# Own tiles for decays and inverses in the first early stage, and its loads in parts

## The chip, the cores and the metric

The kernel runs on one core of one Trainium2 chip. The metric is the device time of one execution in microseconds (us), taken from the kernel's first to its last work on that core; lower is better. Several timed runs are given by their median, and one more execution was profiled.

## The reference

Three stages follow each other. The first is a linear recurrence over 768 steps for 4 x 8 heads with a 40 x 40 state; its output, as 3072 rows of 320, goes through a dense two-layer network and then through a network of 8 experts, where each row goes to the expert with the largest logit.

```python
for t in range(S):                       # S = 768, state: B x H x D x D, D = 40
    y[:, :, t] = einsum('bhd,bhde->bhe', rt, state)
    Sa = einsum('bhde,bhe->bhd', state, at)
    state_decay = state * wt[:, :, None, :] - einsum('bhd,bhe->bhde', Sa, bt)
    state = state_decay + einsum('bhd,bhe->bhde', vt, kt)
x = y.transpose(0, 2, 1, 3).reshape(3072, 320)
h = x @ w_in;  g = maximum(0.01 * h, h);  x = g @ w_out       # 320 -> 2048 -> 320
e = argmax(x @ w_gate, axis=1)                                # 8 experts, capacity 768
out[i] = gate[i] * (relu(x[i] @ w1[e]) @ w2[e])
...
```

The weights w_in and w_out arrive as 64-bit floats; the kernel reads their bits and makes 32-bit floats of them.

## The kernel before

**Stages.** The recurrence is cut into 12 pieces of 64 steps for each half of the heads. `early(e)` (6 of them, e = 0 to 5) prepares four such pieces, `c4` = 0 to 3, for 104 used partitions and 8 head pairs: it loads decays w and the vectors a, b, k (`early_load`, one row of 2057 floats for each of 104 partitions: 521 of w, 512 each of a, b and k), makes running products of the decays with a scan (`eW`, line 439) and of their inverses backwards (`eWi`, line 448), scales a, b and k by them (lines 444, 453, 454), writes the decays, the scaled a, the inverses and the scaled k to DRAM (`dW`, `dA`, `dI`, `dK`: `put`, lines 443, 450, 451, 455), and multiplies b with a on TensorE into `Lt` (lines 463 and 465). When all four pieces are in `Lt`, it inverts the triangular matrices: three transposes (lines 475 and 478), 30 elimination steps of two VectorE instructions each (lines 483 and 485), and a short tail on TensorE into `Inv[e % 2]`.

`late_load(i)` and `late(i)` (48 of them) read back what `early` wrote, for half of the heads of one piece; `chain(i)` carries the state through piece i and writes to `xd`; `moe(v)` (12 of them) is the dense network on 256 rows. `convert` makes 32-bit weights of w_out and w_in chunk by chunk: a load into a ring of three buffers (line 268), one ScalarE step (line 277), four or five VectorE or GpSimd steps (lines 279 to 285) and the split into two parts (290, 391). Behind the last chain come the experts (`Phase2`).

**Around the change.** In `early(0)` all four loads are issued ahead (five transfers, as the third is cut in two). The four pieces share one tile `s.eW` for the decays and one tile `s.eWi` for the inverses; a piece can write them only when the transfers to `dW` and `dI` of the piece before have read them. The raw data lie in `s.eL[0]`, in `s.eL[1]` (the same memory as `P` and `I11`, which the elimination uses), in `s.Inv[1]` and in a tile of the conversion's room `cv`; k of the third piece lies in `s.FG[2]`.

`clear(2)` fills `FG[2]`, `S`, `Inv[0]` and the logits with zeros on GpSimd (lines 225 to 227) and puts identities into `RI` on VectorE (line 231). `beyond` (line 247, ScalarE) looks at the raw decays for values out of range, two passes for each piece, and uses the place of the raw b as its output; in `early(0)` it comes behind the fourth `Lt`. The first transpose writes `P` and so waits for `beyond` of the second piece.

**Order.** Each engine and SP, which issues all of these transfers, works in order. The order on each engine is not that of the source: a planner at compile time ranks instructions by priority and by its own estimate of when each can start, so that the pieces, the late steps and the conversions come interleaved. `ahead(...)` raises the priority of `early(0)` and of the first chains; `issue_after` keeps `clear(2)`, the first late steps and `beyond` behind the last products of piece 3. `run` then merges 46 steps of `early(0)`, 8 of the first two `late`, and the conversion of the first 10 chunks of w_out.

```python
ld = [s.early_load(e, c4) for c4 in range(1 if e else 4)]
fW, fWi, fd = f(s.eW), f(s.eWi), f(s.ed1)
put(s.dW[ch], s.eW[q104])
put(s.dI[ch], s.eWi[q104, :, 1:65])
drain(take(ev, 12))
merge([(ev, 46), (l01, 8), (take(pr, P0), P0)])
```

Of the kernel before, what the change touches and what calls it, by code (L numbers as in the profile page):

```python
# [16 lines left out]
ALU = mybir.AluOpType  # L17
# [31 lines left out]
X0 = 1  # L49
# [35 lines left out]
class Room:  # L85
# [6 lines left out]
    def new(s, sh, dt=F32):  # L92
        s.n += 1
        n = f"{s.name}{s.n}"
        return s.p.tile(sh, dt, name=n, tag=n)
# [35 lines left out]
class Phase1:  # L131
# [272 lines left out]

    def early_load(s, e, c4):
        hh, C = e // 3, 4 * (e % 3) + c4
        t = s.eL0[c4] if e == 0 else s.eL[c4 % 2]
        src = s.I["e_wabk"][C, hh]
        if e == 0 and c4 == 2:
            k = s.FG[2].rearrange("q p two t -> q (p two t)")[0:104, 0:512]  # L410
            s.nc.sync.dma_start(t, src[:, 0:1545])
            s.nc.sync.dma_start(k, src[:, 1545:2057])
        else:
            k = t[:, 1545:2057]
            s.nc.sync.dma_start(t, src)
        v = lambda x: x.rearrange("q (p t) -> q p t", t=64)
        return t[:, 0:521], v(t[:, 521:1033]), v(t[:, 1033:1545]), v(k)

    def early(s, e):
        nc = s.nc  # L420
        ps = lambda: s.psum("m1") if e == 0 else s.psum("se")
        f = lambda t: t[0:104].rearrange("q p t -> q (p t)")
        ld = [s.early_load(e, c4) for c4 in range(1 if e else 4)]
        if e:
            yield
        for c4 in range(4):
            if c4 < 3 and e:
                ld.append(s.early_load(e, c4 + 1))
            ew, ea, eb, ek = ld[c4]
            q104 = slice(0, 104)  # L430
            fW, fWi, fd = f(s.eW), f(s.eWi), f(s.ed1)
            ch = 4 * e + c4
            put = nc.sync.dma_start
            s.clamp(ew, 520)

            if c4 == 0 and e:
                nc.vector.memset(s.ed1[:, :, 0:1], 1.0)
            for h in (0, 260):
                nc.vector.tensor_tensor_scan(fW[:, h:h + 260], ew[q104, h:h + 260], fd[:, h:h + 260], 0.0,
                                             op0=ALU.mult, op1=ALU.add)  # L440
            if c4 < 3:
                nc.vector.tensor_copy(s.ed1[q104, :, 0:1], s.eW[q104, :, 64:65])
            put(s.dW[ch], s.eW[q104])
            m1 = (nc.gpsimd if e or X0 & 1 else nc.vector).tensor_tensor(ea[q104], ea[q104], s.eW[q104, :, 0:64], op=ALU.mult)
            for h in (0, 1):
                c = slice(260 * h, 260 * h + 260)
                nc.vector.reciprocal(s.edr[q104, :, 64:65], s.eW[q104, 4 * h:4 * h + 4, 64:65])
                nc.vector.tensor_tensor_scan(fWi[:, c][:, ::-1], ew[q104, 1:521][:, c][:, ::-1], f(s.edr)[:, ::-1], 0.0,
                                             op0=ALU.mult, op1=ALU.add)
            put(s.dA[ch], ea[q104])  # L450
            put(s.dI[ch], s.eWi[q104, :, 1:65])
            yield
            m2 = (nc.gpsimd if e or X0 & 2 else nc.vector).tensor_tensor(eb[q104], eb[q104], s.eWi[q104, :, 1:65], op=ALU.mult)  # L453
            nc.gpsimd.tensor_tensor(ek[q104], ek[q104], s.eWi[q104, :, 1:65], op=ALU.mult)
            put(s.dK[ch], ek[q104])
            yield
            for _ in range(PD if e else 0):
                yield
            pB = ps().rearrange("q (p t) -> q p t", t=64)
            for p in range(8):  # L460
                for pi in range(2):
                    q = 64 * (1 - pi)
                    m3 = nc.tensor.matmul(pB[q:q + 64, p, :], lhsT=eb[q:q + 40, p, :], rhs=ea[q:q + 40, p, :],  # L463
                                          start=True, stop=True)
            m4 = nc.scalar.mul(s.Lt[:, c4], pB, -1.0)
            s.marks = m1, m2, m3, m4
            if e:
                s.beyond(ew, ch, eb)
            else:
                s.ew0.append((ew, eb))  # L470
            yield
# [8 lines left out]
        for j in range(1, 31):  # L480
# [3 lines left out]
                                    op=ALU.mult)  # L484
# [18 lines left out]
        for c in range(4):  # L503
            v = ps()[:, 0:256].rearrange("q (p t) -> q p t", t=32)
# [7 lines left out]
            v = ps()[:, 0:256].rearrange("q (p t) -> q p t", t=32)  # L512
# [217 lines left out]
    def run(s, p2):  # L730
# [25 lines left out]
        ev = ahead(s.tc, s.early(0), HE, HL, 52)  # L756
        room, wT, wg = s.room(0)
        i1 = s.Inv[1].rearrange("q c p t -> q (c p t)")
        s.eL0 = s.eL + [i1[0:104, 0:1545], s.chip.left[-1].new([104, 2057])]
        pr = s.convert(room, s.wout_chunks(wT, wg, s.banks["m2"], range(0, P0 + P1)))  # L760
        q = ExitStack()
        s.ew0 = []
# [674 lines left out]
```

## Time and profile before

| | |
|---|---|
| timed runs | 1274.09, 1274.45, 1287.01 us; median 1274.45 |
| the profiled execution, its own time | 1275.27 us |
| its span, first to last instruction | 1273.6 us |
| TensorE matmul busy | 1037.1 us, 81% of the span |
| VectorE (DVE) busy | 800.0 us, 63% |
| ScalarE (ACT) busy | 511.8 us, 40% |
| GpSimd (POOL) busy | 408.0 us, 32% |
| TensorE clock granted, mean | 0.942 of 2.4 GHz |
| moved by DMA | 149.52 MB, 117 GB/s over the span |

A busy share is a mean over stages with different limits, so a table by stretches of time is read with it. In a timeline a row is one instruction, or several alike in succession: its start, its length, engine, line of the code, operation, output and input; in brackets stands how long the engine had been idle before it and what it then was released by. SPq is the queue that issues transfers; its rows are the time of issuing, not of the transfer. "p", "cv" and the like are the rooms in which tiles lie, not single tiles.

### The profile page before, as it was taken

Reading aid. Unit: us, or ns where it says so; the run is one execution under the profiler, and the core shown is the slowest. Engines: PE = TensorE matmul, PEld = TensorE weight load, DVE = VectorE, ACT = ScalarE, POOL = GpSimd, SP = SyncE. Lnnn points to the kernel's source line nnn. Section 1 sums busy time; section 2 is a strip of 40 time slices with the busy share of each in tenths; the row PEclk is TensorE's granted clock in tenths of the full one; section 3 lists DMA queues with packets and bytes.
Section 4 is the critical chain, followed back from the end, with each engine's and each line's share of the span. In section 5 each row is a group of like instructions: output and inputs, shape, how many; then the busy total and the mean of one; then the engine's idle time right before and its main releaser. Section 6 shows DMA issues by size and latency. Waiting matters only on the chain. (4 is left out here: it accounts for less than half of the span.)

```text
span 1273.6 us, 31259 instructions
## 1 busy us (share of the span) xinstructions
PE 1037.1 (81%) x12429; PEld 937.0 (74%) x12429; DVE 800.0 (63%) x1677; ACT 511.8 (40%) x1113; POOL 408.0 (32%) x458
## 2 busy tenths in 40 slices
PE   1348943599889989898979988999998968979994
PEld 1336732478778878787878878889898958878983
DVE  4698597894696558855884579544368445543541
ACT  1334442345435354455434543444443235332330
POOL 3364453444321332234222332122242321432210
PEclk9999999999998989998987989999999988989998
DMA  6665265347534654466434644233233444533100
GB/s 166 155 169 138 76 170 153 110 100 181 147 93 101 151 148 104 108 163 162 104 102 105 166 118 113 71 96 91 73 110 103 132 125 126 183 104 106 32 21 20
DMA packets 215735, 149.52 MB, mean 117 GB/s; under 512 B 152820, under 2 KB 195979, under 8 KB 213061
## 3 DMA queue, kind: packets, MB, share of 16 engines
q1 hardware_dynamic: 211949, 138.47, 41.7%
q0 software_dynamic: 3504, 7.75, 2.0%
q8 instruction: 122, 2.00, 0.7%
q14 instruction: 160, 1.31, 0.4%
HBM read 112.39 MB, written 37.21 MB: 117 GB/s over the span
## 5 line engine op out<-in xcount | busy, mean ns | idle before, releaser
L707 PE MATMUL bank<-w,m 128*128 128x328 f32 x792 | 151.2, 329 | 1.6 <-ACT m L691 1.3
L1123 PE MATMUL bank<-p,p 128*128 128x256 f32 (+1 forms) x704 | 121.5, 332 | 33.3 <-issue 26.9
L1123 PEld LDWEIGHTS bank<-p,p 128*128 128x128 f32 x704 | 113.8, 208 | 37.8 <-issue 30.0
L686 PE MATMUL bank<-m,w 128*128 128x256 f32 x768 | 125.0, 309 | 7.2 <-DVE m L690 7.1
L707 PEld LDWEIGHTS bank<-w,m 128*128 128x128 f32 x792 | 122.2, 193 | 9.7 <-issue 2.5
L690 DVE TENSOR_TENSOR m<-bank,m 128x512 f32<-128x512 f32 x96 | 66.8, 696 | 87.5 <-ACT m L689 87.0
L686 PEld LDWEIGHTS bank<-m,w 128*128 128x128 f32 x768 | 106.5, 205 | 14.8 <-DVE m L690 7.6
L686 PE MATMUL bank<-g,w 128*128 128x256 f32 x768 | 114.9, 298 | 0.0
L693 POOL TENSOR_TENSOR m<-m,m 128x128 fp32r<-128x128 f32 x66 | 46.1, 699 | 192.1 <-ACT m L691 185.0
L686 PEld LDWEIGHTS bank<-g,w 128*128 128x128 f32 x768 | 101.4, 198 | 5.5 <-issue 2.0
L572 POOL TENSOR_SCALAR_AFFINE_SELECT p<-p 64x512 f32<-64x512 f32 x94 | 67.3, 716 | 104.4 <-ACT p L570 102.5
L689 ACT ACTIVATE m<-bank 128x512 f32<-128x512 f32 x96 | 57.2, 596 | 96.9 <-PE bank L686 66.7
L1140 PE MATMUL bank<-p,p 128*128 128x320 f32 x600 | 93.3, 311 | 0.0
L1140 PEld LDWEIGHTS bank<-p,p 128*128 128x128 f32 x600 | 88.5, 188 | 0.0
L463 PE MATMUL bank<-p 40*64 40x64 f32 x736 | 35.7, 262 | 57.0 <-POOL p L453 22.2
L485 DVE TENSOR_TENSOR p<-p 128x30 f32<-128x30 f32 (+9 forms) x180 | 74.1, 412 | 3.5
L463 PEld LDWEIGHTS bank<-p 40*64 40x64 f32 x736 | 32.1, 172 | 60.1 <-issue 25.6
L1146 POOL DMA_INDIRECT out<-p,p x25 | 25.0, 999 | 156.5 <-DVE p L1145 114.9
L483 DVE TENSOR_TENSOR p<-p 128x30 f32<-128x30 f32 (+9 forms) x180 | 69.5, 386 | 3.2
L707 PE MATMUL bank<-w,g 128*128 128x328 f32 x360 | 70.2, 340 | 0.0
L612 DVE TENSOR_TENSOR p<-bank,p 64x256 f32<-64x256 f32 x94 | 39.6, 421 | 46.5 <-PE bank L607 30.6
L1126 ACT ACTIVATE p<-bank 128x384 fp32r<-128x384 f32 (+2 forms) x88 | 36.3, 415 | 78.3 <-PE bank L1123 66.0
(234 smaller groups left out, 2199.4 us busy)
## 6 DMA issues: line engine op xcount, KB each, us to landing
p<-in_e_wabk SPq DMA_DIRECT2D x22, 835.7 KB
p<-in_w SPq DMA_DIRECT2D x8, 1280.0 KB
p<-di SPq DMA_DIRECT2D x96, 104.0 KB
p<-in_w SPq DMA_DIRECT2D x8, 1024.0 KB
p<-in_t_kb SPq DMA_DIRECT2D x48, 160.0 KB
dw<-p SPq DMA_DIRECT2D x24, 211.2 KB
di<-p SPq DMA_DIRECT2D x24, 208.0 KB
p<-dk SPq DMA_DIRECT2D x48, 104.0 KB
```

The source lines that it names most:

```text
L463: m3 = nc.tensor.matmul(pB[q:q + 64, p, :], lhsT=eb[q:q + 40, p, :], rhs=ea[q:q + 40, p, :], start=True, stop=True)
L483: nc.vector.tensor_tensor(tm, bc(P[:, j + 1:32, j:j + 1], [128, n, j]), bc(P[:, j:j + 1, 0:j], [128, n, j]), op=ALU.mult)
L485: s.step = nc.vector.tensor_tensor(P[:, j + 1:32, 0:j], P[:, j + 1:32, 0:j], tm, op=ALU.add)
L572: nc.gpsimd.affine_select(out=Fv, in_=Fv, compare_op=ALU.is_gt, fill=0.0, base=0, pattern=[[0, 4], [0, 2], [1, 64]], channel_multiplier=-1)
L612: nc.vector.tensor_tensor(F[q:q + 64, :, pi, 64:128], x[q:q + 64, :, 0:64], bc(s.nmask[q:q + 64, None, :], [64, 4, 64]), op=ALU.mult)
L686: nc.tensor.matmul(o, lhsT=l, rhs=r, start=(n == 0), stop=(n == 7))
L689: nc.scalar.mul(g, ph, 0.01)
L690: nc.vector.tensor_tensor(g, ph, g, op=ALU.max)
L693: nc.gpsimd.tensor_tensor(gL[:, GS:512], g[:, GS:512], gH[:, GS:512], op=ALU.subtract)
L707: nc.tensor.matmul(po[tt], lhsT=l[:, ts], rhs=r[:, fc, :], start=(fc == 0 and n == 0), stop=(fc == NFC - 1 and n == 2))
L1123: nc.tensor.matmul(o, lhsT=l, rhs=r, start=(i == 0), stop=(i == 7))
L1140: nc.tensor.matmul(po, lhsT=l[:, ts], rhs=r[:, fc, :], start=(fc == 0 and i == 0), stop=(fc == 7 and i == 2))
```

## The change

In `early(0)`, and only there, each piece gets a place of its own for the decays and for the inverses (`s.eW0`): piece 0 keeps `s.eW` and `s.eWi`, the decays of pieces 1 to 3 lie in `s.Inv[0]`, the inverses of pieces 1 and 2 in `s.FG[2]` and of piece 3 in a new tile. The scans, the products and the transfers to DRAM of a piece use its own place. `s.ed1` and `s.edr` stay shared.

The loads of the four pieces are cut into three parts each: w (521 floats a row), a and b together (1024), and k (512). The w and the a-and-b part of all four pieces are issued first, eight transfers, and then the four k parts: twelve transfers in place of five, of the same bytes. The raw data of pieces 2 and 3 move: piece 2 into a new tile and `Inv[1]`, piece 3 into a new tile and `Inv[1]`. The code for e = 1 to 5, the late steps, the chain and the conversions stay as they are.

```diff
--- before.py
+++ after.py
@@ -404,23 +404,27 @@
 
     def early_load(s, e, c4):
         hh, C = e // 3, 4 * (e % 3) + c4
-        t = s.eL0[c4] if e == 0 else s.eL[c4 % 2]
         src = s.I["e_wabk"][C, hh]
-        if e == 0 and c4 == 2:
-            k = s.FG[2].rearrange("q p two t -> q (p two t)")[0:104, 0:512]
-            s.nc.sync.dma_start(t, src[:, 0:1545])
-            s.nc.sync.dma_start(k, src[:, 1545:2057])
+        if e == 0:
+
+            w, ab, k = s.eL0[c4]
+            s.nc.sync.dma_start(w, src[:, 0:521])
+            s.nc.sync.dma_start(ab, src[:, 521:1545])
         else:
-            k = t[:, 1545:2057]
+            t = s.eL[c4 % 2]
+            w, ab, k = t[:, 0:521], t[:, 521:1545], t[:, 1545:2057]
             s.nc.sync.dma_start(t, src)
         v = lambda x: x.rearrange("q (p t) -> q p t", t=64)
-        return t[:, 0:521], v(t[:, 521:1033]), v(t[:, 1033:1545]), v(k)
+        return w, v(ab[:, 0:512]), v(ab[:, 512:1024]), v(k)
 
     def early(s, e):
         nc = s.nc
         ps = lambda: s.psum("m1") if e == 0 else s.psum("se")
         f = lambda t: t[0:104].rearrange("q p t -> q (p t)")
         ld = [s.early_load(e, c4) for c4 in range(1 if e else 4)]
+        if e == 0:
+            for c4 in range(4):
+                nc.sync.dma_start(s.eL0[c4][2], s.I["e_wabk"][c4, 0][:, 1545:2057])
         if e:
             yield
         for c4 in range(4):
@@ -428,7 +432,8 @@
                 ld.append(s.early_load(e, c4 + 1))
             ew, ea, eb, ek = ld[c4]
             q104 = slice(0, 104)
-            fW, fWi, fd = f(s.eW), f(s.eWi), f(s.ed1)
+            eW, eWi = (s.eW, s.eWi) if e else s.eW0[c4]
+            fW, fWi, fd = f(eW), f(eWi), f(s.ed1)
             ch = 4 * e + c4
             put = nc.sync.dma_start
             s.clamp(ew, 520)
@@ -439,19 +444,19 @@
                 nc.vector.tensor_tensor_scan(fW[:, h:h + 260], ew[q104, h:h + 260], fd[:, h:h + 260], 0.0,
                                              op0=ALU.mult, op1=ALU.add)
             if c4 < 3:
-                nc.vector.tensor_copy(s.ed1[q104, :, 0:1], s.eW[q104, :, 64:65])
-            put(s.dW[ch], s.eW[q104])
-            m1 = (nc.gpsimd if e or X0 & 1 else nc.vector).tensor_tensor(ea[q104], ea[q104], s.eW[q104, :, 0:64], op=ALU.mult)
+                nc.vector.tensor_copy(s.ed1[q104, :, 0:1], eW[q104, :, 64:65])
+            put(s.dW[ch], eW[q104])
+            m1 = (nc.gpsimd if e or X0 & 1 else nc.vector).tensor_tensor(ea[q104], ea[q104], eW[q104, :, 0:64], op=ALU.mult)
             for h in (0, 1):
                 c = slice(260 * h, 260 * h + 260)
-                nc.vector.reciprocal(s.edr[q104, :, 64:65], s.eW[q104, 4 * h:4 * h + 4, 64:65])
+                nc.vector.reciprocal(s.edr[q104, :, 64:65], eW[q104, 4 * h:4 * h + 4, 64:65])
                 nc.vector.tensor_tensor_scan(fWi[:, c][:, ::-1], ew[q104, 1:521][:, c][:, ::-1], f(s.edr)[:, ::-1], 0.0,
                                              op0=ALU.mult, op1=ALU.add)
             put(s.dA[ch], ea[q104])
-            put(s.dI[ch], s.eWi[q104, :, 1:65])
-            yield
-            m2 = (nc.gpsimd if e or X0 & 2 else nc.vector).tensor_tensor(eb[q104], eb[q104], s.eWi[q104, :, 1:65], op=ALU.mult)
-            nc.gpsimd.tensor_tensor(ek[q104], ek[q104], s.eWi[q104, :, 1:65], op=ALU.mult)
+            put(s.dI[ch], eWi[q104, :, 1:65])
+            yield
+            m2 = (nc.gpsimd if e or X0 & 2 else nc.vector).tensor_tensor(eb[q104], eb[q104], eWi[q104, :, 1:65], op=ALU.mult)
+            nc.gpsimd.tensor_tensor(ek[q104], ek[q104], eWi[q104, :, 1:65], op=ALU.mult)
             put(s.dK[ch], ek[q104])
             yield
             for _ in range(PD if e else 0):
@@ -756,7 +761,16 @@
         ev = ahead(s.tc, s.early(0), HE, HL, 52)
         room, wT, wg = s.room(0)
         i1 = s.Inv[1].rearrange("q c p t -> q (c p t)")
-        s.eL0 = s.eL + [i1[0:104, 0:1545], s.chip.left[-1].new([104, 2057])]
+        new = s.chip.left[-1].new
+        i0 = s.Inv[0].rearrange("q c p t -> q (c p t)")
+        fg = s.FG[2].rearrange("q p two t -> q (p two t)")
+        w = lambda x: x.rearrange("q (p t) -> q p t", t=65)
+        cut = lambda t: (t[:, 0:521], t[:, 521:1545], t[:, 1545:2057])
+        t3 = new([104, 1545])
+        s.eL0 = [cut(s.eL[0]), cut(s.eL[1]), (new([104, 521]), i1[0:104, 0:1024], i1[0:104, 1024:1536]),
+                 (t3[:, 0:521], t3[:, 521:1545], i1[0:104, 1536:2048])]
+        s.eW0 = [(s.eW, s.eWi)] + [(w(i0[:, 520 * k:520 * k + 520]), x) for k, x in
+                                   enumerate((w(fg[:, 0:520]), w(fg[:, 520:1040]), new([128, 8, 65])))]
         pr = s.convert(room, s.wout_chunks(wT, wg, s.banks["m2"], range(0, P0 + P1)))
         q = ExitStack()
         s.ew0 = []
```

## Rows read from the trace of the kernel before

**Rows 1.** Busy time by stretches; columns as the first line says
```profile
core 0: us, PE busy (x) PEld busy (x) DVE busy (x) ACT busy (x) POOL busy (x), PEclk, DMA share, GB/s
0.00:52.00 52.00, 11.27 (x180) 10.33 (x180) 23.46 (x43) 8.94 (x16) 17.93 (x29) 1.00 0.65 159
52.00:102.00 50.00, 24.38 (x132) 19.23 (x128) 47.19 (x120) 20.22 (x60) 26.97 (x24) 1.00 0.70 185
...
600.00:700.00 100.00, 89.50 (x1252) 78.59 (x1254) 73.47 (x148) 40.63 (x87) 26.51 (x30) 0.86 0.42 103
...
800.00:900.00 100.00, 97.92 (x1554) 87.95 (x1547) 46.09 (x90) 50.00 (x107) 23.67 (x30) 1.00 0.38 94
```

**Rows 2.** Timeline of DVE, 0 to 64 us
```profile
7.97 0.43 DVE L242 TENSOR_SCALAR p<-p 104x512 f32<-104x512 f32 x1 [7.97 <-DMA p<-in_e_wabk]
...
12.59 0.43 DVE L242 TENSOR_SCALAR p<-p 104x512 f32<-104x512 f32 x1 [3.38 <-DMA p<-in_e_wabk]
...
16.60 1.40 DVE L242 TENSOR_SCALAR p<-p 104x512 f32<-104x512 f32 x1
21.14 0.43 DVE L242 TENSOR_SCALAR cv<-cv 104x512 f32<-104x512 f32 x1 [3.14 <-DMA cv<-in_e_wabk]
...
32.15 0.70 DVE L439 TENSOR_TENSOR_SCAN p<-cv,p 104x260 f32<-104x260 f32 x1 [2.45 <-DMA dw<-p]
34.76 0.70 DVE L448 TENSOR_TENSOR_SCAN p<-p,p 104x260 f32<-104x260 f32 x1 [1.92 <-DMA di<-p]
...
44.02 0.70 DVE L448 TENSOR_TENSOR_SCAN p<-cv,p 104x260 f32<-104x260 f32 x1 [5.41 <-DMA di<-p]
...
45.70 0.69 DVE L453 TENSOR_TENSOR cv<-cv,p 104x512 f32<-104x512 f32 x1
...
52.11 1.94 DVE L475 STREAM_TRANSPOSE p<-p 128x1024 f32<-128x1024 f32 x1 [2.07 <-ACT p L247]
...
61.12 0.32 DVE L280 TENSOR_SCALAR cv<-cv 128x320 uint32<-128x320 uint32 x1
```

**Rows 3.** Groups of instructions by line and shape, 0 to 52 us
```profile
L231 DVE COPY p<-all 40x160 f32<-40x160 f32 x6 | 2.4, 400 | 0.1
...
L447 DVE RECIPROCAL p<-p 104x4 f32<-104x4 f32 x8 | 1.3, 168 | 0.1
```

**Rows 4.** Timeline of POOL, 0 to 52 us
```profile
16.03 1.68 POOL L454 TENSOR_TENSOR p<-p,p 104x512 f32<-104x512 f32 x1 [0.63 <-DVE p L448]
23.90 1.17 POOL L444 TENSOR_TENSOR p<-p,p 104x512 f32<-104x512 f32 x1 [6.19 <-DVE p L447]
...
42.07 1.22 POOL L225 MEMSET p<- 128x1344 f32 x1 [0.24 <-DMA dk<-p]
45.74 1.68 POOL L454 TENSOR_TENSOR cv<-cv,p 104x512 f32<-104x512 f32 x1 [2.46 <-DVE p L448]
```

**Rows 5.** Timeline of SP, 0 to 54 us
```profile
0.83 0.81 SPq L415 DMA_DIRECT2D p<-in_e_wabk  x2
...
31.11 0.90 SPq L451 DMA_DIRECT2D di<-p  x1
...
47.45 0.31 SPq L455 DMA_DIRECT2D dk<-cv  x1
...
53.39 1.30 SPq L268 DMA_DIRECT2D cv<-in_w_out  x3
```

**Rows 6.** Timeline of ACT, the first conversion of w_out
```profile
57.88 0.49 ACT L277 ACTIVATE cv<-cv 128x320 f32<-128x320 f32 x1 [0.99 <-DMA cv<-in_w_out]
```

**Rows 7.** Busy time by stretches of 10 us; columns as in group 1
```profile
50.00:60.00 10.00, 3.96 (x58) 3.20 (x52) 7.67 (x12) 7.83 (x20) 2.37 (x3) 1.00 0.80 207
...
90.00:100.00 10.00, 5.64 (x23) 4.47 (x23) 10.00 (x32) 3.40 (x12) 5.53 (x5) 1.00 0.98 238
```

**Rows 8.** Timeline of DVE, pieces 1 and 2 of the second early stage
```profile
175.41 0.41 DVE L242 TENSOR_SCALAR p<-p 104x512 f32<-104x512 f32 x1
...
188.07 0.42 DVE L242 TENSOR_SCALAR p<-p 104x512 f32<-104x512 f32 x1
```

## The prediction

> **What bounds the kernel now.** I read the busy table by stretches first, then the timelines of the engines at the front. From 600 us on TensorE is busy 90 to 98% of the time; in the first 52 us it is busy 11 us, and VectorE, which leads there, only 23.46 of 52 [rows 1]. From 52 to 102 VectorE is busy 47.19 of 50 us. So the front is a stretch of waits, what follows is a stretch of VectorE's work, and later TensorE sets the pace. Nothing in the program is tied to a point of time: all later work starts from what the first early stage leaves behind, so a microsecond won at the front is carried to the end unless something on the way is not ready earlier.
>
> VectorE's timeline shows what it waits for [rows 2]. First the loads: 7.97, 3.38 and 3.14 us ahead of three clamps. Then the stores: 2.45 us for a transfer to `dW`, 1.92 and 5.41 us for transfers to `dI`; that is the one tile for all pieces, read by the transfer while the next scan wants to write it. The last product of the stage ends at 45.70 + 0.69 = 46.39, the first transpose starts at 52.11, behind the products, `Lt` and `beyond` on ScalarE. The three later stores cost 9.8 us, and they also push the scans apart so that the loads and the stores alternate.
>
> **What the change removes: the waits for stores.** With a place for each piece no scan waits for a store. What remains is VectorE's own work: 23.46 us busy in the stretch less 2.4 us for the identities, 21.1 us, or 5.3 a piece [rows 1, 3]. That is measured with GpSimd beside it.
>
> **The loads in parts.** Two whole loads end 12.59 - 7.97 = 4.62 us apart [rows 2], for 2057 floats a row. The first w alone (521 floats) is there (1536/2057) x 4.62 = 3.45 us earlier, at 4.5. A piece without k takes 3.47 us, so the fourth w is there at 14.9 and its a and b at 17.2; the k parts follow, 1.15 us each, to 21.8. VectorE reaches piece 3 at 4.5 + 3 x 5.3 = 20.4: from piece 1 on the loads are ahead of it. Twelve issues instead of five cost some 0.4 us each on SP [rows 5], 5 us in all, done before the first store can be ready; nothing waits for that. The stage ends at 4.5 + 21.1 = 25.6 in place of 46.39: 20.8 us. Should the first w land no sooner than now, the stage ends at 29.1, 17.3 us earlier; the next part shows why that may not matter.
>
> **The tail of the stage** (products, `Lt`, `beyond`, then the transpose at 52.11) keeps its 5.7 us: the last product leaves VectorE for TensorE and ScalarE as before, and `P` still lies where the second piece was loaded. The identities (2.4 us) stay hidden in it. The transposes would start 20.8 us earlier, at 31.3.
>
> **What is late next: the conversion of w_out.** VectorE's list has conversion steps between the elimination steps, the first at 61.12 [rows 2]. Moved by 20.8 us it is due at 40.3. Its data come by SP, issued at 53.39, in ScalarE's hands at 57.88 [rows 5, 6]. Two things hold that transfer. SP issues it 5.94 us behind the last `dK` store, which follows the last product with k on GpSimd: ready at 25.0, 1.68 us [rows 4], so 26.7, then 5.9 and 4.5 us as now: 37.1 at the earliest. And the transfers queued ahead of it must have moved: 159 GB/s over 52 us, 8.27 MB [rows 1]. From 1.2 us on, with 0.33 MB for the chunk itself, that lasts to 47.7 at the rate of the loads (0.86 MB in 4.62 us, 185 GB/s), to 42.8 at 207 GB/s, and to 37.3 at 238 GB/s [rows 7]. I take 207, because in that stretch the very same late loads were moving; 238 belongs to a stretch with the large writes of zeros. So the chunk comes at 42.8, 57.88 - 42.8 = 15.1 us earlier than now (10.2 to 20.6), and the first VectorE step on it 15.1 us earlier than 61.12, at 46.0, where VectorE would stand since 40.3. VectorE works in order, so the 5.7 us are lost, and 15.1 us go on.
>
> **New waits.** `clear(2)` now must wait for more: `FG[2]` holds inverses and `Inv[0]` decays, so the zeros come behind `dI` of pieces 1 and 2 and `dW` of 1 to 3. Now the filling of `FG[2]` waits 0.24 us, and the last product with k is queued behind it on GpSimd [rows 4]. A store to `dI` is followed 3.65 us after its issue by the scan that waited for it [rows 2, 5]. Piece 2's inverses are ready at 4.5 + 3 x 5.3 = 20.4; stored at once, 24.1 and the last product waits for nothing. With the queue of transfers ahead (the loads to 21.8, then nine stores, 1.9 MB, 9.2 us at 207 GB/s) it is 31.0: the last product then ends at 31.0 + 1.22 + 1.68 = 33.9 instead of 26.7, and the w_out chunk may come at 37.1 + 7.2 = 44.3 instead of 42.8. That is 0 to 1.5 us; I take 0, since the first store of piece 2 is not the last of nine. If nothing else held the chunk back, it would cost 7.2. The k parts, last in line, delay products with k and `dK`, not the scans; the late loads that need `dK` lie in the same queue, already counted.
>
> **The sum.** Profiled execution 1275.27 us, less 15.1: 1260.2. The median of the three runs shown is 0.8 lower, which would give 1259.4; I say 1260.
>
> **Rivals.**
> *All of it is carried.* If the planner lets the elimination run alone until the chunk is there, VectorE does not stand: 20.8 us, 1254.5. For it: the elimination has the higher priority. Against it: now the first conversion step comes 9 us behind the first transpose, and the order is fixed before the run.
>
> *VectorE and GpSimd get in each other's way.* A clamp took 1.40 us where a GpSimd product of 1.68 us had begun just before it, and 0.43 alone [rows 2, 4]. Packed more tightly, they meet more often. Bare, VectorE's stage is 4 x 0.43 + 16 x 0.70 + 1.3 + 4 x 0.69 = 17.0 us [rows 2, 3], GpSimd's eight products 4 x (1.17 + 1.68) = 11.4 [rows 4]; one after the other 28.4, the stage ends at 32.9, 13.5 us earlier, and the chunk is there by then: 1261.8. The Trainium skill has such a rule (SBUF — State Buffer, section "Who interferes with whom"): a VectorE instruction with two SBUF inputs and a GpSimd instruction that reads SBUF exclude each other for their whole length. The clamp's row agrees: the page counts operations of its kind in where they run in a mode with two ports. The 21.1 us of the sum lie between the full price, 28.4, and none, 17.0.
>
> *The gain is given back in the second early stage.* Its pieces come about 12.7 us apart [rows 8], with loads between those of w_in in SP's queue. If the new order puts one of them a round later, 12.7 of 15.1 us are gone: 1272.9. For it: the whole order is planned anew, with rings and priorities that were set for the old one. Against it: that stage's code is the same.
>
> *Slower: TensorE's clock.* In the TensorE part the granted clock was 0.86 at 89.5 us of work in 100 and 1.00 at 97.9 [rows 1], between its two levels, 1.2 and 2.4 GHz. A mean lower by 0.01 costs up to 1037.1 x 0.01 / 0.942 = 11 us. From 0.014 lower on the kernel is slower than before; 0.020 gives 1282. For it: the third run shown, 12.6 us above the median, and a stage that is packed differently from its start. Against it: the work there and its order within a step do not change.
>
> *The change does not do what it says.* If the scans still wait, for instance because the planner puts them behind other work for which stores are needed, only the earlier first w remains: 3.45 us, 1271.8.
>
> **How the numbers follow.** Forecast 0.45 (its own range 1254.7 to 1265.1, by the two transfer rates), all carried 0.17, in each other's way 0.10, given back 0.13, slower clock 0.11, not what it says 0.04. 1% is 12.7 us and about what a measurement of this kernel can tell from none: the bounds are 1261.7 and 1287.2. Faster by more: all carried, and of the forecast and of the collision what lies below 1261.7, 0.28 and 0.04: 0.49. Slower by more: the clock case beyond 0.025, 0.07 with what I can't name. The rest, 0.44, within 1%. The range leaves out the clock case and the far end of the case with all carried: 1250 to 1277.
>
> **What would show it.** VectorE in the first 30 us: no wait for `dw` or `di`, first clamp near 4.5, last product near 25.6, first transpose near 31. Then a wait for w_out (or for the steps on it) of some 6 us on VectorE at 40 to 46; if it isn't there, all is carried. Scans of 1.3 us and more beside GpSimd products show the collision; clamps of the second early stage further than 12.7 us apart the gain given back; a mean clock below 0.93 the clock. The prediction is wrong if VectorE's waits only change their name, or if the elimination ends 15 us earlier and the last chain step doesn't.

## The result and the profile after

| | before | after |
|---|---|---|
| timed beside each other, median of four | 1275.84 us | 1295.78 us |
| lowest and highest | 1274.09, 1287.01 | 1292.54, 1299.47 |
| profiled execution, its own time and span | 1275.27, 1273.6 | 1293.12, 1291.4 |
| TensorE clock granted, mean | 0.942 | 0.891 |

The changed kernel is slower: ratio 1.012, 95% interval 1.007 to 1.0165 (the quotient of the two medians is 1.016). I had predicted 1260 us, with a range of 1250 to 1277.

**The front, VectorE.** Below is VectorE's timeline of the changed kernel.

```profile
4.29 0.43 DVE L242 TENSOR_SCALAR p<-p 104x512 f32<-104x512 f32 x1 [4.29 <-DMA p<-in_e_wabk]
7.20 0.43 DVE L242 TENSOR_SCALAR p<-p 104x512 f32<-104x512 f32 x1 [2.49 <-DMA p<-in_e_wabk]
10.27 0.43 DVE L242 TENSOR_SCALAR cv<-cv 104x512 f32<-104x512 f32 x1 [2.63 <-DMA cv<-in_e_wabk]
10.61 1.28 DVE L444 TENSOR_TENSOR_SCAN p<-p,p 104x260 f32<-104x260 f32 x2
...
30.95 0.69 DVE L458 TENSOR_TENSOR cv<-cv,cv 104x512 f32<-104x512 f32 x1
...
37.41 1.97 DVE L480 STREAM_TRANSPOSE p<-p 128x1024 f32<-128x1024 f32 x1 [3.95 <-ACT p L247]
...
66.38 0.18 DVE L490 TENSOR_TENSOR p<-p 128x30 f32<-128x30 f32 x1
```

Against [rows 2]: no scan waits for a store any more, and the last product ends at 31.64 instead of 46.39. The transposes start 14.7 us earlier. The last elimination step (L490, 66.38) is 33.4 us earlier than in the kernel before, where this row of its VectorE timeline is the same step:

```profile
99.77 0.19 DVE L485 TENSOR_TENSOR p<-p 128x30 f32<-128x30 f32 x1
```

SP's and GpSimd's timelines of the changed kernel show what did not move (SP's rows are times of issue):

```profile
4.73 0.47 SPq L427 DMA_DIRECT2D p<-in_e_wabk  x1
14.84 0.31 SPq L448 DMA_DIRECT2D dw<-p  x1
15.19 0.38 SPq L427 DMA_DIRECT2D p<-in_e_wabk  x1
...
34.74 1.43 SPq L427 DMA_DIRECT2D p<-in_e_wabk  x1
...
40.58 0.32 SPq L460 DMA_DIRECT2D dk<-p  x1
...
42.09 0.99 SPq L535 DMA_DIRECT2D p<-di  x2
...
53.18 0.40 SPq L553 DMA_DIRECT2D p<-dw  x1
53.62 1.30 SPq L268 DMA_DIRECT2D cv<-in_w_out  x3
```

```profile
38.19 1.22 POOL L225 MEMSET p<- 128x1344 f32 x1 [6.10 <-DMA di<-p]
39.37 1.18 POOL L459 TENSOR_TENSOR p<-p,cv 104x512 f32<-104x512 f32 x1
```

The first loads of w_out are issued at 53.62, before at 53.39 [rows 5]. VectorE's first step on w_out starts at 66.15, before at 61.12 [rows 2]; by then all 60 instructions of the elimination but the last are done.

**How far the gain got.** Each chain copies its X once on ScalarE; I count these copies from 0 and take the end of copy k as the end of chain k. These are copies 7, 16, 32 and 47, first of the kernel before, then of the changed one (ScalarE's timelines):

```profile
285.52 0.51 ACT L602 COPY p<-bank 128x416 f32<-128x416 f32 x1 [1.56 <-PE bank L601]
...
442.88 0.51 ACT L602 COPY p<-bank 128x416 f32<-128x416 f32 x1 [1.88 <-PE bank L601]
...
714.48 0.51 ACT L602 COPY p<-bank 128x416 f32<-128x416 f32 x1 [0.30 <-PE bank L601]
...
933.33 0.51 ACT L602 COPY p<-bank 128x416 f32<-128x416 f32 x1 [0.76 <-PE bank L601]
```

```profile
279.83 0.51 ACT L607 COPY p<-bank 128x416 f32<-128x416 f32 x1 [1.50 <-PE bank L606]
...
435.97 0.51 ACT L607 COPY p<-bank 128x416 f32<-128x416 f32 x1 [1.88 <-PE bank L606]
...
727.13 0.51 ACT L607 COPY p<-bank 128x416 f32<-128x416 f32 x1 [1.89 <-PE bank L606]
...
949.66 0.51 ACT L607 COPY p<-bank 128x416 f32<-128x416 f32 x1 [0.76 <-PE bank L606]
```

Of 33.4 us, 5.7 are left at chain 7 and 6.9 at chain 16. Then 19.6 us are lost between chains 16 and 32 and 3.7 more up to chain 47. These are figures of one execution each: in a second profile of the changed kernel (after_again below, the same order on VectorE, ScalarE and SP) chain 7's copy starts at 285.97, no earlier than in the kernel before, and chains 16 to 32 lose 14.8 us. So there are two questions: where the front's gain went, and where the later loss comes from. From some 824 us on (VectorE's list) both kernels have the same order, and the distance stays (16.3 us at chain 47, 16.2 at the start of the experts); before that the whole order is another one.

**One step that stands elsewhere.** `run` writes zeros to `out` with four transfers of 960 KB, written in the source at chain 16 and bound to nothing else. SP's timelines, before and after, with the loads of `early(3)`:

```profile
93.41 7.63 SPq L815 DMA_DIRECT2D out<-p  x3
...
411.73 0.39 SPq L415 DMA_DIRECT2D p<-in_e_wabk  x1
```

```profile
409.77 0.42 SPq L829 DMA_DIRECT2D out<-p  x1
419.21 0.53 SPq L829 DMA_DIRECT2D out<-p  x1
424.52 0.41 SPq L829 DMA_DIRECT2D out<-p  x1
430.18 0.60 SPq L829 DMA_DIRECT2D out<-p  x1
434.28 0.84 SPq L416 DMA_DIRECT2D p<-in_e_wabk  x2
```

Three of them ran at 93 us before, in the very stretch of 238 GB/s in [rows 7]; now all four stand ahead of the loads of `early(3)`, and its first clamp (VectorE's first step on a piece) starts at 443.43 instead of 418.61. VectorE, before and after:

```profile
418.61 0.43 DVE L242 TENSOR_SCALAR p<-p 104x512 f32<-104x512 f32 x1 [0.98 <-DMA p<-in_e_wabk]
```

```profile
443.43 0.43 DVE L242 TENSOR_SCALAR p<-p 104x512 f32<-104x512 f32 x1
```

### The profile page after: what moved, and what is told of

Its sections match the earlier page's. It is cut to its first block, busy times and chain, and to the rows that moved or that the text cites. A ratio compares the mean times of both kernels' runs of the same rounds, so it can differ in the third digit from the quotient of the medians.

```text
span 1291.4 us, 31249 instructions
## 1 busy us (share of the span) xinstructions
PE 1051.0 (81%) x12429; PEld 948.9 (73%) x12429; DVE 807.5 (63%) x1677; ACT 513.5 (40%) x1113; POOL 404.6 (31%) x458
## 5 line engine op out<-in xcount | busy, mean ns | idle before, releaser
L712 PE MATMUL bank<-w,m 128*128 128x328 f32 x792 | 161.4, 342 | 1.4 <-ACT m L696 1.3
L1137 PEld LDWEIGHTS bank<-p,p 128*128 128x128 f32 x704 | 114.2, 210 | 39.6 <-issue 30.0
L712 PEld LDWEIGHTS bank<-w,m 128*128 128x128 f32 x792 | 128.6, 201 | 10.3 <-issue 2.7
L698 POOL TENSOR_TENSOR m<-m,m 128x128 fp32r<-128x128 f32 x66 | 48.7, 738 | 248.3 <-ACT m L696 230.3
L490 DVE TENSOR_TENSOR p<-p 128x30 f32<-128x30 f32 (+9 forms) x180 | 70.2, 390 | 4.2
L712 PE MATMUL bank<-w,g 128*128 128x328 f32 x360 | 67.0, 327 | 0.0
L600 ACT COPY p<-bank 40x416 f32<-40x416 f32 x94 | 47.0, 500 | 49.8 <-PE bank L596 48.0
```

What stands on the lines that cost most here:

```text
L490: s.step = nc.vector.tensor_tensor(P[:, j + 1:32, 0:j], P[:, j + 1:32, 0:j], tm, op=ALU.add)
L600: nc.scalar.copy(F[q:q + 40, :, pi, 64:168], y[q:q + 40])
L698: nc.gpsimd.tensor_tensor(gL[:, GS:512], g[:, GS:512], gH[:, GS:512], op=ALU.subtract)
L712: nc.tensor.matmul(po[tt], lhsT=l[:, ts], rhs=r[:, fc, :], start=(fc == 0 and n == 0), stop=(fc == NFC - 1 and n == 2))
L1137: nc.tensor.matmul(o, lhsT=l, rhs=r, start=(i == 0), stop=(i == 7))
```

## The experiments

Times are given as ratio to the kernel before, measured on the same chip, with the 95% interval; medians of the kernel before were 1278 to 1285 us there. Theories: **A**, the conversions of w_out and w_in, not the first early stage, set the end of the first 280 us. **B**, the later loss belongs to the new order, not to the front. **D**, it is the zero transfers themselves. **E**, it is the order that the planner builds around them. What was expected of each kernel stands in the order in which the kernels are named.

**Front and order taken apart.** A barrier over all engines ahead of chain 8 makes the planner start alike behind it; the two kernels, before_b8 and after_b8, then have one order there.

```diff
             if i == 8:
+                s.tc.strict_bb_all_engine_barrier()
```

> The kernel before with one barrier over all engines ahead of chain 8 (some 300 us into the span). Behind a barrier the planner starts from the same state, so this kernel and the next have the same order on every engine behind it. No theory needs a number here but as the base of the next: the barrier drains what overlaps chain 7 and 8, estimated at 0 to 15 us, so 1275 to 1290 us.

> The changed kernel with the same barrier. The profiles of both kernels show chain 8 ended 2.6 us earlier with the change, the last piece of w_in 8.5 us earlier. If the change itself gains a little and the later order loses it (theory B), this kernel is 2 to 9 us below the one before it with the same barrier. If the front itself or the slower TensorE clock in 137 to 239 us costs the time, it is 10 to 20 us above. By my prediction's sum it would be 15 us below.

Measured: 1.030 (1.020 to 1.039) and 1.024 (1.016 to 1.032). In the profiles chain 8 ends 7.1 us earlier with the change, chain 47 7.8 us: with one order the front's gain is carried, at 7 us, not 15. The timed runs cannot tell the two kernels apart, and the barrier itself cost some 34 us by the medians, where 0 to 15 had been expected. And the kernel before, given only a barrier, itself takes 291.1 us from chain 16 to 32, as the changed kernel does (271.6 in its own order): B.

**Each half of the change alone.** Own tiles with the loads in six transfers (tiles_only, the first four lines), and the loads in parts with the shared tiles (parts_only, the last two):

```diff
-            s.nc.sync.dma_start(w, src[:, 0:521])
-            s.nc.sync.dma_start(ab, src[:, 521:1545])
+            if c4 < 2:
+                s.nc.sync.dma_start(s.eL[c4], src)
...
-            eW, eWi = (s.eW, s.eWi) if e else s.eW0[c4]
+            eW, eWi = s.eW, s.eWi
```

> The own tiles of the changed kernel, but its loads nearly whole, in six transfers where the changed kernel has twelve. Its order behind the second early stage is that of the changed kernel, step by step. Theory B (the later order loses the time): within 6 us of the changed kernel, 1290 to 1302 us, and as late as it from early(3) on. If the loads in parts and their places in SP's queue were the cause: back to the kernel before or under it, 1262 to 1277 us.

> The loads in parts of the changed kernel, with the shared tiles of the kernel before. Its order on TensorE is that of the kernel before to the last instruction, on the other engines from the front on. Theory B: within 5 us of the kernel before, 1270 to 1281 us, nothing lost between 440 and 810 us. If twelve loads instead of five were what costs the time: 1288 to 1302 us.

Measured: 1.009 (1.005 to 1.013) and 1.000 (0.996 to 1.004). The own tiles bring the loss and move the zero transfers (416 us); the loads in parts leave the zeros at 93 us and cost nothing.

**Front and order crossed.** Every engine is tied to a given order, from chain 8 on, by ordering edges that wait for nothing. The kernels are new_front_old_order, old_front_new_order and, with no edit, after_again:

```diff
             if i == 8:
+                first = len(s.nc.cur_bb.bb.instructions)
...
+        given_order(s.tc, s.nc, first)
```

> The changed kernel, whose instructions from the eighth chain on (8470 of them, some 300 us into the span) are tied on each engine to the order that they had in the kernel before. Theory B (the change itself wins a little, the new order of 440 to 810 us loses some 20 us): 4 to 9 us below the kernel before, chains 16 to 32 in some 272 to 279 us as in the kernel before (291 us in the changed kernel). If the front or the granted clock behind it costs the time, whatever the order: 10 to 20 us above the kernel before. By my prediction's sum: 15 us below.

> The kernel before, tied in the same way to the order of the changed kernel from the eighth chain on. Theory B: 15 to 28 us above the kernel before, chains 16 to 32 in 286 to 293 us. If the front costs the time: within 5 us of the kernel before.

> The changed kernel once more, beside the two that cross its front and its order: 1290 to 1300 us, 10 to 20 us above the kernel before in the runs beside it.

Measured: 1.011 (1.007 to 1.015), 1.015 (1.008 to 1.022), 1.018 (1.012 to 1.024). Chains 16 to 32 took 273.9, 288.9 and 286.4 us: that stretch goes with the order. (after_again lies some 23 us above the kernel before, a little more than expected.) But the first kernel missed the gain that theory B expected of it, since the seam failed: chain 8 came 33.3 us behind chain 7 (18.3 before). Its ScalarE and SP show why:

```profile
313.54 0.83 ACT L722 CAST g<-m 128x768 fp32r<-128x768 f32 x1 [16.72 <-DMA m<-xd]
314.27 0.50 ACT L661 COPY p<-bank 128x416 f32<-128x416 f32 x1
```

```profile
278.99 0.41 SPq L884 DMA_DIRECT2D out<-p  x1
...
288.59 1.63 SPq L884 DMA_DIRECT2D out<-p  x2
290.27 4.50 SPq L470 DMA_DIRECT2D p<-in_e_wabk  x1
303.75 0.34 SPq L502 DMA_DIRECT2D dw<-p  x1
...
309.23 0.39 SPq L718 DMA_DIRECT2D m<-xd  x1
```

The old order had the zeros ahead of these, at 93 us; in the new front there was no such place, and three came at 279 to 290, the fourth at 318. The issue behind them, a load of raw data for `early(2)`, took 4.50 us; the store to `dW` made from that data went out at 303.75 only, and the load for the dense network (L718) stood behind it in the same queue. ScalarE waited for that load 16.72 us, and chain 8's copy stood behind that on ScalarE. The second kernel answers theory A: with the old front, whose last elimination step starts at 100.22, chain 7's copy starts at 279.43, no later than in the changed kernel (279.83), where that step is 33.8 us earlier. VectorE, then ScalarE, of old_front_new_order:

```profile
100.22 0.19 DVE L544 TENSOR_TENSOR p<-p 128x30 f32<-128x30 f32 x1
```

```profile
279.43 0.51 ACT L661 COPY p<-bank 128x416 f32<-128x416 f32 x1 [1.56 <-PE bank L660]
```

The early stage did not set the pace. (TensorE's order in this kernel is not that of the kernel before from some 131 us on, so the order alone can be worth these 6 us too.) What chain 7 goes with is the last load of w_in: in ten of the thirteen profiles with own tiles chain 7's copy starts 31.9 to 32.3 us behind its issue, be that at 237.96 or at 259.07 us, with the last elimination step anywhere between 65.9 and 80.0. The other three are tiles_only (39.6), w_first_zero_early below (37.8) and after_again (37.8, by the clock, as the part on it shows).

**w_out first.** On the first of these kernels (w_out_first):

```diff
         drain(take(ev, 12))
+        with s.tc.high_priority(offset=100):
+            next(pr)
```

> The first kernel of this group (new front, old order), with the first chunk of w_out raised in priority: its three loads are the first that SP issues, ahead of the raw data of early(0), and its steps stand between the scans. The first three loads (128 x 640 floats each, 983 KB, some 5 us at the 207 GB/s of rows 7) make the first clamp some 5 us later. If the conversions set the end of the first 270 us (theory A): the last w_in piece and chain 8 come 3 to 15 us earlier than in new_front_old_order, and so does the end. If the first early stage still sets it: 3 to 6 us later than new_front_old_order.

Measured: 1.007 (1.0035 to 1.011). In the profiles chains 7, 8 and 47 end 4.9, 4.6 and 8.4 us earlier than in new_front_old_order, the first clamp 3 us later: A, at the lower end of what it expected. The times alone, 1.007 and 1.011, lie within each other's intervals.

**The zeros moved, with and without a new plan.** First SP's list alone was changed, and all else tied to the kernel's own order from the first instruction on (after_zero_early, before_zero_late, w_first_zero_early):

```diff
-        given_order(s.tc, s.nc, first)
+        given_order(s.tc, s.nc, 0)
```

> The changed kernel, every engine tied to the order that it has there; only the four transfers that fill out with zeros (960 KB each) are moved on SP's queue, from 410 to 430 us (right ahead of the loads of early(3)) to the front, two behind the transfer of dk1 at some 59 us, two behind the loads of early(1) at some 101 us. Theory D (the loss is the place of the zero fills, which the new plan moved from 93 us to 410 us): the first clamp of early(3) is some 20 us earlier, chains 16 to 32 take 272 to 281 us (291 in the changed kernel), and the time is between 12 us below and 2 us above the kernel before. If the new order of the computing steps is the cause: chains 16 to 32 stay at 286 to 292 us and the time at 10 to 20 us above the kernel before.

> The kernel before, every engine tied to its own order; only the four zero fills are moved on SP's queue, from 93 and 307 us to behind the same transfers as in the changed kernel (some 410 to 440 us). Theory D: chains 16 to 32 take 284 to 293 us instead of 272, and the time is 8 to 20 us above the kernel before. If the order of the computing steps is the cause: within 5 us of the kernel before.

> The kernel of w_out_first (new front, old order from the eighth chain on, the first chunk of w_out raised), tied to its own order, with the zero fills moved to the front, two behind dk1's transfer at some 64 us and two behind the loads of early(1) at some 100 us. In w_out_first the fills stood at 274 to 314 us, and chain 8 ended 33 us behind chain 7 where it is 18 us in the kernel before. Theory D: chain 8 within 22 us of chain 7, and the time 5 to 16 us below the kernel before. If the fills don't matter: as w_out_first, some 7 us above the kernel before.

Then one edit of the source on the changed kernel, free of ties (zero_early_free; the same lines at chain 16 are left out):

```diff
         q.close()
+        for n in range(0, 48, 12):
+            s.nc.sync.dma_start(ov[:, n:n + 12, :], bc(s.z[:, None, :], [128, 12, 160]))
```

> The changed kernel with one edit of the source and no ties: the four zero fills are written behind the first early stage instead of at chain 16; the planner puts them on SP at some 59 to 66 us and plans the rest anew. Theory D: 8 us below to 3 us above the kernel before, chains 16 to 32 in 270 to 282 us. If any new plan loses some 20 us in the middle, whatever the fills do: 8 to 20 us above.

Measured: 1.011 (1.006 to 1.015), 1.008 (1.004 to 1.012), 1.002 (0.998 to 1.005), 1.011 (1.006 to 1.015). D falls as the cause in the changed kernel: without the zeros in the way, its order still takes 293.3 us from chain 16 to 32, and its loads of `early(3)` are issued at 435.56, because they are tied. In the kernel before, the same move costs some 10 us, but elsewhere: chain 12 to 16 takes 78.6 instead of 71.9 us. The fourth kernel got the good order (274.9 us) by a new plan, but the zeros at 55 to 84 us delayed w_out: its chain 7 ended at 291.8, 11.5 us later than in the changed kernel. The third won some 7 us of ratio against w_out_first; its chain 8 came 27.5 us behind chain 7, between the 33.6 there and the 22 that D expected at most, so the zeros made some 6 of the 15 us that the seam cost.

**The zeros where they harm nobody, and the converse.** The two edits, on the changed kernel (zero_spread) and on the kernel before (before_zero_behind); w_first_zero_spread has the first of them and that of w_out_first:

```diff
-            if i == 16:
-                for n in range(0, 48, 12):
-                    s.nc.sync.dma_start(ov[:, n:n + 12, :], bc(s.z[:, None, :], [128, 12, 160]))
+            if i in (34, 36, 38, 40):
+                n = 6 * (i - 34)
+                s.nc.sync.dma_start(ov[:, n:n + 12, :], bc(s.z[:, None, :], [128, 12, 160]))
...
             if i == 16:
+                with s.tc.issue_after(prev):
                     for n in range(0, 48, 12):
```

> The changed kernel with one edit of the source and no ties: the four zero fills are written one each at chains 34, 36, 38 and 40 instead of all at chain 16. Its order is that of the changed kernel up to some 290 us; behind that the planner puts the first clamp of early(3) at chain 14 to 15 again. Theory E (the fills ahead of early(3) in the plan push the early stages 1.8 chains back, and that order costs the time): chains 16 to 32 in 268 to 280 us, the gain of the front (some 7 us at chain 16) reaches the end, 3 to 10 us below the kernel before. If a new plan loses the time for another reason: 286 to 293 us there, 10 to 20 us above.

> The kernel before with one edit and no ties: the four zero fills may not be issued ahead of the transfers that are written before them at chain 16, so that the planner cannot put three of them at 93 us. The front is the kernel before's. Theory E: early(4) and early(5) stand some 1.5 chains later in its plan, chains 16 to 32 take 284 to 293 us, and the time is 10 to 20 us above the kernel before. If the new front is needed for the loss: within 5 us of the kernel before, or 8 us above it as with the fills moved alone.

> Both edits on the changed kernel, no ties: the zero fills spread over chains 34 to 40, and the first chunk of w_out raised, so that its loads are issued first. Theory E with theory A: 6 to 14 us below the kernel before, chain 8 at 293 to 299 us. If the w_in conversions give the 5 us back by chain 8: as zero_spread.

Measured: 1.002 (0.998 to 1.005), 1.016 (1.012 to 1.021), 0.995 (0.992 to 0.9985). SP's timeline of zero_spread, then of before_zero_behind:

```profile
407.02 0.40 SPq L416 DMA_DIRECT2D p<-in_e_wabk  x1
...
673.19 0.41 SPq L829 DMA_DIRECT2D out<-p  x1
```

```profile
433.13 0.41 SPq L818 DMA_DIRECT2D out<-p  x1
439.56 4.46 SPq L818 DMA_DIRECT2D out<-p  x3
```

For the stretch of chains 16 to 32 E holds in both directions: the good order comes back, and the kernel before loses its own. Two things it did not foresee. The gain of the front did not reach zero_spread's time (3 to 10 us below were expected). And in before_zero_behind the fills are issued behind the loads of `early(3)`, whose first clamp stays near where it was (14.3, 14.6); only `early(4)` is pushed back. So it is shown that this order costs the time, and that the place given to the fills decides which order comes; by which step of the planner is not. This table puts the orders together; a position is that of the first clamp between the chains' copies (14.6: six tenths from copy 14 to copy 15):

| kernels | zeros issued, us | first clamp of `early(3)`, `early(4)` | chains 16 to 32, us |
|---|---|---|---|
| before | 93, last at 307 | 14.6, 22.5 | 271.6 |
| before_zero_late | 418 to 447 | 14.6, 22.5 | 269.8 |
| new_front_old_order, w_out_first | 274 to 318 | 14.6, 22.5 | 273.9, 270.9 |
| zero_early_free | 55 to 84 | 14.7, 22.5 | 274.9 |
| zero_spread, w_first_zero_spread | 668 to 824 | 14.7, 22.5 | 269.1, 269.9 |
| after, tiles_only | 410 to 439 | 16.4, 24.1 to 24.2 | 291.2, 289.0 |
| after_again, old_front_new_order | 408 to 437 | 16.4, 24.1 | 286.4, 288.9 |
| after_zero_early | 59 to 103 | 16.4, 24.1 | 293.3 |
| before_b8, after_b8 | 431 to 444 | 16.8, 24.1 | 291.1, 289.4 |
| before_zero_behind | 433 to 441 | 14.3, 24.1 | 283.1 |

The time goes with the order (third column), not with the transfers themselves (second): before_zero_late has the zeros late and the old order, after_zero_early has them early and the new one. parts_only, too, has the order of the kernel before here; its one profile is that of the longest of its ten runs, so its 279.1 us are not compared.

The busy table of that stretch, for before, after and zero_spread (columns as in [rows 1]):

```profile
443.40:715.00 271.60, 246.70 (x3558) 219.43 (x3558) 187.26 (x388) 122.83 (x263) 85.82 (x96) 0.91 0.51 127
```

```profile
436.50:727.60 291.10, 261.13 (x3558) 229.99 (x3558) 192.88 (x394) 123.53 (x262) 86.58 (x94) 0.88 0.49 122
```

```profile
436.70:705.70 269.00, 241.56 (x3558) 215.17 (x3557) 187.83 (x388) 122.37 (x262) 82.20 (x94) 0.94 0.52 130
```

The same 3558 matmuls: in the changed order TensorE is idle 30.0 us instead of 24.9, and busy 14.4 us longer at a lower granted clock, 0.88 instead of 0.91. The clock is not the whole of it: after_again took 286.4 us at a mean of 0.91, the same as before, with TensorE idle 33.3 us. Through which step the order costs the time was not taken apart.

**What the front is worth.** Two repeats of kernels above with no further edit (zero_spread_2, w_first_zero_spread_2), and both edits, of w_out and of the zeros, on the kernel before (before_w_first):

> zero_spread once more, beside the next two. Own tiles worth what the profiles show: 3 to 8 us below the kernel before. Worth nothing in the end: within 3 us of it.

> w_first_zero_spread once more: 3 to 9 us below the kernel before, 3 to 7 us below zero_spread_2.

> The kernel before, with shared tiles and whole loads, and the same two edits: first chunk of w_out raised, zero fills written at chains 34 to 40 (the planner still issues two of them at some 93 us and one at 307). If the own tiles are worth their 7 us: 2 us below to 5 us above the kernel before, and 5 to 10 us above w_first_zero_spread_2. If the win of w_first_zero_spread is that of the raised chunk alone: 3 to 9 us below the kernel before.

Measured: 0.9995 (0.995 to 1.004), 0.9985 (0.995 to 1.002), 1.020 (1.013 to 1.026). The own tiles with the zeros out of the way make the time of the kernel before, not less, though chain 47 ends 8.2 and 4.9 us earlier in the profiles. Those profiles are of runs of 1273.02 and 1273.31 us, the shortest and the second shortest of twelve each (medians 1282.52 and 1285.55), so a part of the 8.2 and 4.9 can be the execution; and in the first of them the experts' stage took 258.6 us, 251.4 in the kernel before. With w_out first it was 0.5% faster once and not to be told from the kernel before the second time: 6 and 2 us, where 6 to 14 and 3 to 9 had been expected. Without own tiles the raised chunk costs time, which neither expectation had: the last elimination step is 6 us later than before, and the last step on w_in 2 us. Its profiled run was the shortest of six, 1287.67 us, against a median of 1308.34, so where the rest goes stays open.

## Why the prediction was wrong

**Right.** The waits for stores are gone, the first clamp is at 4.29 (said: 4.5), GpSimd's eight products took the 11.4 us that I had, and the tail from the last product to the transposes took 5.77 us (5.7).

**The stage's length, 21.1 us.** It took 27.35. VectorE was busy 21.9 of these; 5.12 are waits for loads, because the order has the clamps of pieces 1 and 2 ahead of the first scan. I had worked out when data arrive, not in which order VectorE would ask. The rival in which VectorE and GpSimd exclude each other had the end at 32.9, near 31.64, but mostly by luck. Its sign came, scans of 1.46 to 1.70 us beside GpSimd products, four of them; here is one on VectorE and the product beside it:

```profile
22.68 1.69 DVE L453 TENSOR_TENSOR_SCAN p<-p,p 104x260 f32<-104x260 f32 x1
```

```profile
22.65 1.17 POOL L449 TENSOR_TENSOR cv<-cv,p 104x512 f32<-104x512 f32 x1 [1.23 <-DVE p L452]
```

Yet in all VectorE was busy 4.9 us more than its bare 17.0, where the rival had 11.4 more: 21.9 us lie near the sum's 21.1, which had this in it already. The rule of the Trainium skill behind it (SBUF — State Buffer, section "Who interferes with whom") is neither borne out at full price nor excluded by this.

**The twelve issues and the zeros of `FG[2]`.** "Nothing waits for that" was wrong: the second k part is issued right behind the first store to `dW` (15.19), the fourth at 34.74. And the fill of `FG[2]`, which I priced at 0 to 1.5 us, waited 6.10 us for `dI`, with the last product with k behind it: that product began at 39.37, not at 25.0.

**The chunk of w_out, the term that carried the sum.** I had it 15.1 us earlier. Its load was issued 0.23 us later than before, and VectorE's first step on it came at 66.15, not at 46.0: the last `dK` store moved by only 6.9 us (40.58 against 47.45), and 13.0 us instead of 5.9 lie between it and the load. SP issues 23 other transfers in these 13.0 us, most of them loads for the late steps, with no gap over 0.1 us; before, a part of them went out among the stores. I carried a distance between two rows over to a new order, though all the late loads between them were free to move too, and I bounded the load by the bytes ahead of it, not by SP's time to issue.

**"All carried".** This rival's mechanism came, that the elimination runs alone: 33.4 us. Its gain did not, since with an elimination 33.8 us later chain 7 ends at the same time. What ends last there are the conversions, and those did not start earlier (53.62 against 53.39); their last load goes out 3.2 us earlier (247.56 against 250.73).

**"Nothing in the program is tied to a point of time".** This step set the wrong sign. It holds for one order, by the one pair of profiles that shows it (7.1 us at chain 8, 7.8 at chain 47 with the barrier); it does not hold when the planner places anew what is free. I had named the new plan as a rival, at 0.13, with its place in `early(1)` and a price of 12.7 us given back; it struck 300 us later, and cost 14.8 to 19.6 us between chains 16 and 32. Its trigger stood in my own rows: I used the stretch with "the large writes of zeros" as a rate and did not ask what else these transfers could do if they were not issued there. That the own tiles move them is shown (tiles_only); why the planner then found no room at 93 us is not.

**The clock.** This rival's sign came, a mean of 0.891, but not its price: the four runs of the changed kernel had means of 0.891, 0.894, 0.934 and 0.944 and took 1293.12, 1298.43, 1299.47 and 1292.54 us. A mean hides where the clock is low. From 160 to 240 us the changed kernel ran at half the clock throughout; the busy tables of that stretch, before and after:

```profile
160.00:240.00 80.00, 33.13 (x428) 27.41 (x426) 67.41 (x149) 30.04 (x74) 37.67 (x41) 1.00 0.58 151
```

```profile
160.00:240.00 80.00, 32.09 (x380) 27.18 (x381) 67.08 (x149) 26.00 (x64) 37.98 (x40) 0.50 0.53 142
```

TensorE was busy 32 of 80 us there and VectorE 67, and the slower clock cost next to nothing: parts_only, with TensorE in the order of the kernel before, also had 0.50 there, and its chain 7 copy starts at 286.21, 0.7 us later than before. Where TensorE leads it does cost. The changed kernel and after_again, in the same order, TensorE busy all the time in both:

```profile
270.00:280.00 10.00, 9.97 (x190) 8.19 (x189) 6.55 (x12) 5.55 (x14) 1.29 (x2) 1.00 0.48 113
```

```profile
270.00:280.00 10.00, 10.00 (x145) 8.35 (x143) 6.54 (x12) 3.30 (x8) 0.76 (x1) 0.50 0.26 57
```

At 263 us the second is 0.6 us behind, at chain 7's copy 6.1 (279.83 and 285.97). From chain 16 to 32 the new order took 14.8 us more than the old at the same mean, 0.91 (286.4 against 271.6); what the changed kernel's own profile has beyond that, at 0.88, can be the clock's.

## What to carry to other kernels

Where a planner orders the instructions, a local change has two results, its own and a new order, and the second can be the larger: compare the orders, and pin or bar the rest to see the first alone. Large transfers that depend on nothing can wander far (here four of 960 KB, by over 300 us); give them a place in the source where nobody's loads stand behind. And before a stage is made shorter, ask which work ends last behind it: here an elimination 33 us earlier left 6 or 7 us at chain 7 at best, and nothing that the time shows.

## What was not expected of the hardware

- An issue on SP that takes 0.3 to 0.5 us took 4.50 and 4.53 us right behind two transfers of 960 KB (new_front_old_order, w_out_first): the issue itself can be held up, not only the data. A store to `dK` took 4.10 us in before_b8 with none of these transfers near it, so what holds it up stays open.
- Two profiles of the changed kernel, with the same order on VectorE, ScalarE and SP, had the experts' stage in 253.2 and 263.6 us, and 19 runs of the kernel before on one chip lay between 1270.9 and 1290.1 us. A gain of 7 us at chain 47 can be seen in a trace and still not in the time.
